# Window attention and a PReLU feed-forward on one Trainium2 core: the mask of four pairs as an identity product in PSUM, and another order of tile 0's products on TensorE

## The chip, the core and the metric

The kernel runs on one core of a Trainium2 chip. Its engines have queues of their own and run each in program order: TensorE (PE, with the weight loads listed as PEld), VectorE (DVE), ScalarE (ACT), GpSimd (POOL), and SyncE (SP), which here only issues DMAs. [...] The metric is the device time of one execution in microseconds (us); a median of several runs is given. The profile is of one execution.

## What is computed

First attention with a window, for 8 batches, 8 heads, 576 positions and 64 channels a head. The first four heads see the last 32 positions, the other four every fourth of the last 128:

```python
mask_plain = (rel >= 0) & (rel < window)
mask_dil = (rel >= 0) & (rel < window * dilation) & (rel % dilation == 0)
scores = np.where(masks[None, :, :, :], scale * (q @ k.T), -1000000000.0)
attn = softmax(scores)
x = attn @ v            # reshaped to 4608 tokens x 512
```

Then a feed-forward layer on all 4608 tokens, in float32:

```python
h = x @ w_in                                             # 512 -> 2048
g = np.maximum(h, 0.0) + alpha * np.minimum(h, 0.0)
out = g @ w_out                                          # 2048 -> 512
```

## The kernel before

**Attention** is done in 32 *pairs* (a batch and two heads; class `Pair`), four pairs to a batch. Positions are laid out so that both kinds of window become blocks of 32 queries by 64 keys, and a pair is nine such blocks on 128 partitions, 576 columns in all. `scores` makes them on PE into two PSUM banks (five blocks and four). `maxima` (DVE) scales them and adds the mask (L194, out to `pr`), and takes the negative maximum of each row (L197), once for each bank. `exponentials` (ACT, L204) makes nine exponentials with their row sums. `divisions` and `turns` (DVE, L211 to L219) divide and transpose in blocks. `values` (PE, L232) multiplies by the values into two banks. `highs` (ACT, L268) and `lows` (DVE, L273) write the result as a rounded part and the remainder, since every float32 product of the feed-forward is made as three products of such parts.

**The feed-forward** goes through the tokens in tiles of 512 and the 2048 channels in 16 slices of 128. For a slice: `ffn_h` (PE, L341, 12 products) into one bank; `ffn_relu` (ACT, L349 and L350); `ffn_sum` (DVE, L355), which is the last reader of the h bank; `ffn_high` (ACT, L368) and `ffn_low` (DVE, L373) make the two parts of g; `ffn_y` (PE, L388, 12 products) adds into four banks that stay for the tile.

**Weights** come as float64 and are converted: a DMA (L288 or L290), a magnitude on ACT (L308), four word operations on DVE (L314 to L320), then `high` on ACT (L326) and `low` on DVE (L329). There are 32 of them, and the list `wq` gives their order; `taken` says how many conversions are begun at the end of each step. A conversion begun in one step has its words made in the next and its low part in the one after.

**PSUM** has eight banks, under two names: y0 to y3 and a0 to a3. `bank(side, ...)` hands them out in turn, and a new tile in a bank waits for the last reader of the old one. Scores of pairs 0 to 4 (`p <= NC`, with `NC` 4) take y banks, and those of later pairs, all values and all h take a banks.

**The order of the work** is written out by hand, for each engine the order of the calls in the program. At the start, loads of the first pairs, masks and weights are issued. A loop over s = 0 to 3 (the first four pairs) makes maxima and exponentials of pair s, one weight conversion beside them, divisions and transposition, scores of pair s+2 and values of pair s. Then come pair 4's maxima and exponentials and the first two slices' h. A loop over n = 0 to 5 then does slice n of tile 0 (`CUT` 6 slices) beside the scores of pair 5+n and the values of pair 4+n. In a step n of that loop before the change, PE gets: scores of pair 5+n, values of pair 4+n, h of slice n+1, and at the end y of slice n-1. DVE gets: the sum of slice n, maxima of pair 5+n, the low part of slice n, conversion words, lows of pair 4+n, low parts of weights, divisions and transposition of pair 5+n. ACT gets: the cast of slice n, five exponentials of pair 5+n, highs of pair 4+n, the other four exponentials, the relu of slice n+1, casts and magnitudes of weights. After this loop, from n = 6, a loop goes on with tile 1's slices, h of slice n+1 and y of slice n-1 in each step, with no pairs until n = 20. At n = 6 the first six slices' sums are copied out (L398 and L400) through DRAM, and slice 6 starts new ones.

Of the kernel before, what the change touches and what calls it, by code (L numbers as in the profile page):

```python
# [7 lines left out]

F32 = mybir.dt.float32
F32R = mybir.dt.float32r  # L10
U32 = mybir.dt.uint32
AF = mybir.ActivationFunctionType
ALU = mybir.AluOpType

P = 128
# [6 lines left out]
BK = 2 * BQ  # L22
HB = 9
HQ = HB * BQ
CUT0 = 5
# [3 lines left out]
NC = DM // P  # L29
NF = DFF // P  # L30
# [8 lines left out]
CUT = 6  # L39


NMASK = 18
PLAIN, DILATED = 0, 9
NEG = -1.0e30
SCALE = 1.0 / D ** 0.5
# [6 lines left out]
def tile_window_attention_prelu_ffn(  # L52
# [11 lines left out]
    nc = tc.nc  # L64
    PS = bass.MemoryType.PSUM

    const = ctx.enter_context(tc.tile_pool(name="const", bufs=1))
# [9 lines left out]
    mask_sb = const.tile([P, NMASK, BK], F32, name="mask_sb")  # L77
# [11 lines left out]
    def bank(side, shape, name):  # L89
        n = turn[side]  # L90
        turn[side] = n + 1
        return psp.tile(shape, F32, tag=f"{side}{n % 4}", name=name)
# [12 lines left out]
    def place(i, k, dtype=F32R):  # L105
        return const.tile([P, SPANS[k][1] - SPANS[k][0], DM], dtype, tag=f"w{i}_{k}", name=f"w{i}_{k}_{dtype}")

    def weight(which, a, f):
        k = next(k for k in range(3) if f < SPANS[k][1])
        i = 2 * which + a  # L110
        if (i, k) not in places:
            places[i, k] = place(i, k)
        return places[i, k][:, f - SPANS[k][0], :]
# [3 lines left out]
    rooms = [place(i, 2, F32).rearrange("p f n -> p (f n)") for i in range(4)]  # L117
    spare_st = [place(i, 1, U32).rearrange("p f (n w) -> p (f n) w", w=2) for i in range(4)]
    vsize = (HB + 1) * D
    taken = 2 * S + vsize  # L120
    spare_pr = [rooms[i][:, taken:taken + HB * BK].rearrange("p (r k) -> p r k", r=HB) for i in range(2)]
    spare_a = [rooms[i][:, taken:taken + DM].bitcast(U32) for i in (2, 3)]


    cells = {}
# [21 lines left out]
    class Pair:  # L147
        def __init__(self, b, c):
            self.b, self.c = b, c
            p = b * NC + c  # L150
            self.banks = "y" if p <= NC else "a"
            self.plain = 2 * c < HP
            self.mask = PLAIN if self.plain else DILATED
            self.id = f"{b}_{c}"
            self.pr = spare_pr[p % 2] if b < 2 else pr0
            self.room = rooms[c] if b < 2 else None
            self.sm = sums[p % 2]

        def load_qk(self):
# [16 lines left out]
        def scores(self):  # L176


            self.ps = [bank(self.banks, [P, n, BK], f"s_{self.id}_{i}") for i, n in enumerate((CUT0, HB - CUT0))]
            for j in range(HB):  # L180
                for u in range(2):
                    for e in range(2):
                        rows, m, n = slice(e * D, (e + 1) * D), 2 * e + u, u * HB + j
                        keys = self.k[rows, (n - 1) * BQ:(n + 1) * BQ] if n else (
                            self.k[rows, None, :BQ].broadcast_to([D, 2, BQ]))
                        nc.tensor.matmul(  # L186
                            self.ps[j // CUT0][m * BQ:(m + 1) * BQ, j % CUT0, :], lhsT=self.q[rows, n * BQ:(n + 1) * BQ],
                            rhs=keys, start=True, stop=True)

        def maxima(self, between=()):  # L190
            between = list(between)
            self.nm = sml.tile([P, HB], F32, tag="nm", name=f"nm_{self.id}")
            for i, (a, z) in enumerate(((0, CUT0), (CUT0, HB))):
                nc.vector.scalar_tensor_tensor(  # L194
                    out=self.pr[:, a:z], in0=self.ps[i], scalar=SCALE, in1=mask_sb[:, self.mask + a:self.mask + z],
                    op0=ALU.mult, op1=ALU.add)
                nc.vector.tensor_reduce(  # L197
                    out=self.nm[:, a:z], in_=self.pr[:, a:z], axis=mybir.AxisListType.X, op=ALU.max, negate=True)
            for op in between:
                op()  # L200

        def exponentials(self, a=0, z=HB):
            for r in range(a, z):
                nc.scalar.activation(  # L204
                    out=self.pr[:, r, :], in_=self.pr[:, r, :], func=AF.Exp,
                    bias=self.nm[:, r:r + 1], scale=1.0, accum_out=self.sm[:, r:r + 1],
                )

        def divisions(self):
# [126 lines left out]
    def ffn_h(t, f, first=0, end=NC):  # L336
        if first == 0:
            ms[t, f] = bank("a", [P, TT], f"h_{t}_{f}")
        for c in range(first, end):
            for n, (a, e) in enumerate(PASSES):  # L340
                nc.tensor.matmul(  # L341
                    ms[t, f], lhsT=weight(0, a, f)[:, c * P:(c + 1) * P], rhs=half(t, c)[:, e, :],
                    start=(c == 0 and n == 0), stop=(c == NC - 1 and n == 2))

    def ffn_relu(t, f):

        ps = ms[t, f]
        m = ffp.tile([P, TT], F32, tag="m", name=f"m_{t}_{f}", bufs=5)
        nc.scalar.activation(out=m, in_=ps, func=AF.Relu, scale=-1.0)  # L349
        nc.scalar.activation(out=ps, in_=ps, func=AF.Relu)  # L350
        ms[t, f] = ps, m

    def ffn_sum(t, f):
        ps, m = ms[t, f]
        nc.vector.scalar_tensor_tensor(  # L355
            out=m, in0=m, scalar=nal[:, f:f + 1], in1=ps, op0=ALU.mult, op1=ALU.add)
        ms[t, f] = m
# [406 lines left out]
    slices = [(0, f) for f in range(CUT)] + [(1, f) for f in range(NF)] + [(0, f) for f in range(CUT, NF)]  # L764
# [5 lines left out]


    wq = [(0, 0), (0, 1), (1, 0)]
    for f in range(1, NF):
        wq += [(0, f + 1), (1, f)] if f + 1 < NF else [(1, f)]
    order.update({w: i for i, w in enumerate(wq)})
    loads, convs = list(wq), list(wq)

    def load():
        if loads:
            load_weight(*loads.pop(0))  # L780

    def conversion():

        w = Conversion(*convs.pop(0))
        w.magnitude()
        return w
# [17 lines left out]
    pairs[2].load_v()  # L804
    pairs[3].load_v()
    pairs[0].scores()
    pairs[1].scores()
    before = conversion()
    for op in before.words():
        op()  # L810
    before.high()
    for s in range(NC):
        u = pairs[s]
        pairs[s + NC].load_qk()
        load()
        if s == 0:
            u.maxima()
            u.exponentials(0, 3)
            w = conversion()
            u.exponentials(3)  # L820
            nc.vector.tensor_scalar_mul(nal, al, -1.0)
            nc.vector.tensor_scalar(out=bal, in0=al, scalar1=-1.0, scalar2=1.0, op0=ALU.mult, op1=ALU.add)
            for op in w.words():
                op()
            before.low()
        else:
            u.maxima(w.words())
            u.exponentials()
            pairs[s - 1].highs()
        w.high()  # L830
        u.divisions()
        if s + 1 == NC:
            ffn_h(0, 0, 0, 2)
        u.turns()
        later = conversion()
        if s + 2 <= NC:
            pairs[s + 2].scores()
        if s:
            pairs[s - 1].lows()
        w.low()  # L840
        w = later
        u.values()
        pairs[s + NC].load_v()
# [15 lines left out]
    load()  # L859
    late, now = [w], [conversion()]  # L860

    taken = [1, 2, 1, 1, 1, 2] + [1, 1, 2, 1, 1, 1, 2, 1, 1, 2, 1, 2, 1]

    def ahead():
        while taken and len(convs) - taken[0] < len(loads):
# [2 lines left out]
    for n in range(CUT):  # L868
        scored = pairs[NC + 1 + n] if n + 1 < NC else None
        valued = pairs[NC + n] if n < NC else None  # L870
        if n == 0:
            for f in range(2):
                ffn_sum(*slices[f])
            valued.divisions()
            valued.turns()
        elif n > 1:
            ffn_sum(*slices[n])
        if scored:
            scored.scores()
        if valued:  # L880
            valued.values()
        if n:
            ffn_h(*slices[n + 1])
        ffn_high(*slices[n])
        if scored:
            scored.maxima()
            scored.exponentials(0, 5)
        ffn_low(*slices[n])
        if valued:
            valued.highs()  # L890
        if scored:
            scored.exponentials(5)
        if n:
            ffn_relu(*slices[n + 1])
        for w in now:
            for op in w.words():
                op()
        if valued:
            valued.lows()
        for w in late:  # L900
            w.low()
        if scored:
            scored.divisions()
            scored.turns()
        for w in now:
            w.high()
        late, now = now, [conversion() for _ in range(taken.pop(0))]
        ahead()
        if n:
            ffn_y(*slices[n - 1])  # L910

    score_at, value_at = {}, {}
    for p in range(2 * NC, AHEAD):
        n = EARLY + 2 * (p - 2 * NC)
# [5 lines left out]
    for k in range(NFP):  # L920
        n = SCRATCH + 1 + 2 * k + (2 if k > 1 else 0)
# [143 lines left out]
```

## Time and profile before

| | |
|---|---|
| median of 3 runs | 895.48 us (895.02 to 897.18) |
| the profiled execution | 895.02 us, span 892.9 us |
| mean granted TensorE clock | 0.98 |
| busy: PE, PEld | 853.4 us (96% of the span), 706.5 us (79%) |
| busy: DVE, ACT, POOL | 561.3 us (63%), 394.3 us (44%), 46.9 us (5%) |
| DMA, mean over the span | 170 GB/s |

Busy shares are means over stages that differ. The page also cuts the span into 40 slices of 22.3 us each, and there PE is busy for 4, 6, 6 and 8 tenths in the first four, and for nine or more in nearly all others. A row of the timeline gives start, length, engine, line, operation, what is written and read, and in brackets the idle time of the engine before it and what ended it. "Issue" there is a wait for which the profile shows no releaser.

### The profile page before, as it was taken

The numbers are of one execution on the slowest core, as the hardware profiler recorded it, in microseconds if no ns is written. First come the engines' busy times: TensorE is split into PE (matmuls) and PEld (weight loads), VectorE is DVE, ScalarE is ACT, GpSimd is POOL, SyncE is SP. The second block draws the span as 40 slices with busy tenths as digits, with TensorE's granted clock in tenths as the row PEclk, the third lists the DMA queues.
The fourth block names the chain that finished last, engine by engine and source line by source line (L and its number), as shares of the span: only waits on it lengthen the run. The fifth ranks groups of instructions, "written<-read, shape, count | busy, mean of one in ns | idle before, by whom it ended". The sixth has DMA issues, their size and how long they took to land.

```text
span 892.9 us, 19710 instructions
## 1 busy us (share of the span) xinstructions
PE 853.4 (96%) x8048; PEld 706.5 (79%) x8048; DVE 561.3 (63%) x964; ACT 394.3 (44%) x1118; POOL 46.9 (5%) x52
## 2 busy tenths in 40 slices
PE   4668999999999999999999999999999999999998
PEld 4556888888888788888888878888788888888886
DVE  6988799976767677675437655764366537304721
ACT  5566466542533444464336442653255226204600
POOL 0000000020223350000000000000000000000000
PEclk9669999999999999999999999999999999999999
DMA  9612245216889965565556555655365466436631
GB/s 344 219 59 94 86 151 174 80 47 193 253 273 334 301 201 175 188 190 162 156 166 193 173 178 174 195 162 162 96 192 158 148 179 194 124 98 172 180 128 47
DMA packets 101448, 151.81 MB, mean 170 GB/s; under 512 B 8432, under 2 KB 47344, under 8 KB 101360
## 3 DMA queue, kind: packets, MB, share of 16 engines
q1 hardware_dynamic: 101360, 150.58, 54.9%
q8 instruction: 63, 1.03, 0.5%
q14 instruction: 25, 0.20, 0.1%
HBM read 116.99 MB, written 33.55 MB: 169 GB/s over the span
## 4 chain that ended last, share of the span: by engine, by line
PE 94%; DVE 2%; issue 2%; ACT 1%; DMA 0%; SPq 0%; DVEq 0%; ACTq 0%
PE y L676 30%; PE h L341 15%; PE pA L538 15%; PE y L388 15%; PE pC L538 7%; PE o L232 5%; PE pB L538 4%; PE s L186 3%; ACT w_dt.float L204 1%; DMA ws<-w_in 0%; DVE pt L219 0%; DVE w_dt.float L213 0%; DVE w_dt.float32r L329 0%; DVE nm L197 0%; DVE wa L318 0%
## 5 line engine op out<-in xcount | busy, mean ns | idle before, releaser
L341 PE MATMUL h<-x,w_dt.float32r 128*128 128x512 f32 x576 | 144.4, 400 | 1.6 <-issue 1.6
L388 PE MATMUL y<-g,w_dt.float32r 128*128 128x512 f32 x576 | 138.4, 389 | 0.0
L341 PEld LDWEIGHTS h<-x,w_dt.float32r 128*128 128x128 f32 x576 | 109.6, 193 | 25.2 <-issue 1.8
L388 PEld LDWEIGHTS y<-g,w_dt.float32r 128*128 128x128 f32 x576 | 108.0, 188 | 22.5
L676 PE MATMUL y<-gp,ring_w 128*128 128x512 f32 x480 | 112.3, 390 | 0.0
L676 PEld LDWEIGHTS y<-gp,ring_w 128*128 128x128 f32 x480 | 89.7, 188 | 18.9
L676 PE MATMUL y<-gp,ring_xA 128*128 128x512 f32 x444 | 103.8, 390 | 0.0
L676 PEld LDWEIGHTS y<-gp,ring_xA 128*128 128x128 f32 x444 | 83.0, 188 | 17.5
L204 ACT ACTIVATE pr<-pr,nm 128x64 f32<-128x64 f32 x216 | 72.2, 336 | 47.2 <-DVE nm L197 47.2
L580 ACT COPY stage<-pA 128x512 f32<-128x512 f32 x72 | 42.3, 587 | 105.2 <-PE pA L538 105.2
L606 DVE TENSOR_TENSOR gp<-n,gp 128x512 fp32r<-128x512 f32 x96 | 63.1, 683 | 0.0
L368 ACT CAST g<-m 128x512 fp32r<-128x512 f32 x48 | 29.7, 619 | 75.4 <-DVE m L363 69.2
L598 DVE SCALAR_TENSOR_TENSOR n<-n,bal,stage 128x512 f32<-128x512 f32 x72 | 53.9, 748 | 13.6 <-ACT n L594 12.8
L538 PE MATMUL pA<-parts_w,ring_w 128*128 128x512 f32 x234 | 57.7, 390 | 0.7 <-ACT raw_xA L268 0.7
L602 ACT CAST gp<-n 128x512 fp32r<-128x512 f32 x96 | 56.6, 615 | 1.8 <-DVE n L598 1.8
L538 PE MATMUL pA<-parts_w,ring_xA 128*128 128x512 f32 x228 | 56.2, 390 | 0.5 <-ACT raw_xB L268 0.5
L676 PE MATMUL y<-gp,ring_g 128*128 128x512 f32 x228 | 54.5, 391 | 0.0
L699 DVE TENSOR_TENSOR ob<-y,py 128x512 f32<-128x512 f32 x24 | 16.4, 690 | 57.8 <-PE y L676 57.8
L538 PEld LDWEIGHTS pA<-parts_w,ring_w 128*128 128x128 f32 x234 | 43.9, 188 | 9.9 <-ACT raw_xA L268 0.8
L594 ACT ACTIVATE n<-stage 128x512 f32<-128x512 f32 x72 | 45.6, 633 | 12.5 <-DVE stage L587 11.9
L538 PEld LDWEIGHTS pA<-parts_w,ring_xA 128*128 128x128 f32 x228 | 42.7, 188 | 9.5 <-ACT raw_xB L268 0.6
L676 PEld LDWEIGHTS y<-gp,ring_g 128*128 128x128 f32 x228 | 42.5, 188 | 9.1
(97 smaller groups left out, 1147.3 us busy)
## 6 DMA issues: line engine op xcount, KB each, us to landing
ring_w<-wS SPq DMA_DIRECT2D x68, 256.0 KB, 2.9
ring_xA<-wS SPq DMA_DIRECT2D x67, 256.0 KB, 2.9
ring_w<-wO SPq DMA_DIRECT2D x40, 256.0 KB, 2.7
ring_xA<-wO SPq DMA_DIRECT2D x37, 256.0 KB, 2.7
out<-ob SPq DMA_DIRECT2D x36, 256.0 KB, 2.9
ring_g<-wS SPq DMA_DIRECT2D x33, 256.0 KB, 2.9
wO<-w_dt.float32r SPq DMA_DIRECT2D x32, 256.0 KB, 5.0
wS<-wc SPq DMA_DIRECT2D x16, 512.0 KB, 3.7
```

The source lines that it names most:

```text
L204: nc.scalar.activation(out=self.pr[:, r, :], in_=self.pr[:, r, :], func=AF.Exp, bias=self.nm[:, r:r + 1], scale=1.0, accum_out=self.sm[:, ...
L232: nc.tensor.matmul(self.po[u][e * D:(e + 1) * D, a:z, :], lhsT=self.v[rows, i, :], rhs=self.pt[rows, a * BK + (BQ if i else 0):z * BK - (B ...
L341: nc.tensor.matmul(ms[t, f], lhsT=weight(0, a, f)[:, c * P:(c + 1) * P], rhs=half(t, c)[:, e, :], start=(c == 0 and n == 0), stop=(c == NC ...
L368: nc.scalar.copy(out=g[:, 0, :], in_=ms[t, f])
L388: nc.tensor.matmul(ys[t][c], lhsT=weight(1, a, f)[:, c * P:(c + 1) * P], rhs=g[:, e, :], start=(first and n == 0), stop=(last and n == 2),)
L538: nc.tensor.matmul(to, lhsT=w[:, (2 * a + c) * P:(2 * a + c + 1) * P], rhs=part_of(name, e)[:, c * TT:(c + 1) * TT], start=start and c == ...
L580: nc.scalar.copy(out=self.s(n), in_=self.A)
L594: nc.scalar.activation(out=self.m[n], in_=self.at(n), func=AF.Relu, scale=-1.0)
L598: nc.vector.scalar_tensor_tensor(out=self.m[n], in0=self.m[n], scalar=bal[:, f:f + 1], in1=self.at(n), op0=ALU.mult, op1=ALU.add)
L602: nc.scalar.copy(out=self.g(n)[:, 0], in_=self.m[n])
L606: nc.vector.tensor_tensor(out=g[:, 1], in0=self.m.pop(n), in1=g[:, 0].bitcast(F32), op=ALU.subtract)
L676: nc.tensor.matmul(ys2[tt], lhsT=w[:, k * P:(k + 1) * P], rhs=g[:, e], start=j == 0 and n == 0, stop=j == GF - 1 and n == 2)
```

## The change

It has two parts.

*The mask.* For pairs 1 to 4 (`self.onto`) the mask isn't added on DVE. It is written once as rounded float32 (`added`, two copies on ACT), an identity matrix is made on POOL and copied on ACT (`unit_r`), and a product of the two opens each score bank; the score products then add to it. The maxima are taken from PSUM and multiplied by the scale afterwards (two small operations more), and the exponentials read PSUM and write `pr`. So the y banks of these pairs are held until their exponentials have been read.

*The order.* In step n of the loop over tile 0's slices, PE now gets scores of pair 5+n, y of slice n-1, h of slice n+2, and then the values of pair 4+n. The sum on DVE and the relu on ACT are issued for slices n+1 and n+2. The order of the weights and the number of conversions begun in the first steps follow.

```diff
+    added_all = const.tile([P, NMASK + 2, BK], F32R, tag="xC0", name="added")
+    added = {kind: added_all[:, kind:kind + HB] for kind in (PLAIN, DILATED)}
+    unit_r = added_all[:, NMASK:].rearrange("p j k -> p (j k)")
+    unit = rooms[0][:, taken + HB * BK:taken + HB * BK + P]
+    make_identity(nc, unit)
...
+            self.onto = 1 <= p <= NC
...
+            if self.onto:
+                for i, (a, z) in enumerate(((0, CUT0), (CUT0, HB))):
+                    nc.tensor.matmul(
+                        self.ps[i], lhsT=unit_r, rhs=added[self.mask][:, a:z],
+                        start=True, stop=False, skip_group_check=True)
...
-                            rhs=keys, start=True, stop=True)
+                            rhs=keys, start=not self.onto, stop=True, skip_group_check=self.onto)
...
-                nc.vector.scalar_tensor_tensor(
-                    out=self.pr[:, a:z], in0=self.ps[i], scalar=SCALE, in1=mask_sb[:, self.mask + a:self.mask + z],
-                    op0=ALU.mult, op1=ALU.add)
+                if not self.onto:
+                    nc.vector.scalar_tensor_tensor(
+                        out=self.pr[:, a:z], in0=self.ps[i], scalar=SCALE, in1=mask_sb[:, self.mask + a:self.mask + z],
+                        op0=ALU.mult, op1=ALU.add)
                 nc.vector.tensor_reduce(
-                    out=self.nm[:, a:z], in_=self.pr[:, a:z], axis=mybir.AxisListType.X, op=ALU.max, negate=True)
+                    out=self.nm[:, a:z], in_=self.ps[i] if self.onto else self.pr[:, a:z],
+                    axis=mybir.AxisListType.X, op=ALU.max, negate=True)
+                if self.onto:
+                    nc.vector.tensor_scalar_mul(self.nm[:, a:z], self.nm[:, a:z], SCALE)
...
-                    out=self.pr[:, r, :], in_=self.pr[:, r, :], func=AF.Exp,
-                    bias=self.nm[:, r:r + 1], scale=1.0, accum_out=self.sm[:, r:r + 1],
+                    out=self.pr[:, r, :], in_=self.ps[r // CUT0][:, r % CUT0, :] if self.onto else self.pr[:, r, :],
+                    func=AF.Exp, bias=self.nm[:, r:r + 1], scale=SCALE if self.onto else 1.0,
+                    accum_out=self.sm[:, r:r + 1],
...
-    for f in range(1, NF):
-        wq += [(0, f + 1), (1, f)] if f + 1 < NF else [(1, f)]
+    wq += [(0, 2), (0, 3), (1, 1), (0, 4), (1, 2), (0, 5), (1, 3), (1, 4), (1, 5)]
+    for f in range(CUT, NF):
+        wq += [(0, f), (1, f)]
...
     pairs[0].scores()
+    before = conversion()
+    nc.scalar.copy(out=unit_r, in_=unit)
+    nc.scalar.copy(out=added[PLAIN], in_=mask_sb[:, PLAIN:PLAIN + HB])
     pairs[1].scores()
-    before = conversion()
...
         later = conversion()
+        if s == 0:
+            nc.scalar.copy(out=added[DILATED], in_=mask_sb[:, DILATED:DILATED + HB])
...
-    taken = [1, 2, 1, 1, 1, 2] + [1, 1, 2, 1, 1, 1, 2, 1, 1, 2, 1, 2, 1]
+    taken = [2, 1, 1, 1, 1, 2] + [1, 1, 2, 1, 1, 1, 2, 1, 1, 2, 1, 2, 1]
...
         if n == 0:
-            for f in range(2):
-                ffn_sum(*slices[f])
+            ffn_sum(*slices[0])
+            ffn_sum(*slices[1])
             valued.divisions()
             valued.turns()
-        elif n > 1:
-            ffn_sum(*slices[n])
+        elif n + 1 < CUT:
+            ffn_sum(*slices[n + 1])
         if scored:
             scored.scores()
+        if n:
+            ffn_y(*slices[n - 1])
+        if n + 2 <= CUT:
+            ffn_h(*slices[n + 2])
         if valued:
             valued.values()
-        if n:
-            ffn_h(*slices[n + 1])
         ffn_high(*slices[n])
...
-        if n:
-            ffn_relu(*slices[n + 1])
+        if n + 2 <= CUT:
+            ffn_relu(*slices[n + 2])
...
         ahead()
-        if n:
-            ffn_y(*slices[n - 1])
```

`make_identity` is a helper: a memset and an `affine_select` on POOL.

More of the change, by code (lines that the diff above doesn't have):

```diff
@@ L7 @@
 from concourse._compat import with_exitstack
+from concourse.masks import make_identity
 F32 = mybir.dt.float32
```

## The prediction

> **What bounds the kernel now.** I read the header of the page first, then a table of the windows at the start, then the chain of waits over the first 150 us.
>
> ```profile
> span 892.9 us, 19710 instructions
> ```
>
> The profiled execution took 895.02 us, 2.1 us more than its span; the median of the three runs is 895.48 us. My sum is a shift of the profiled execution, and what lies around the span stays as it is.
>
> ```profile
> 50.00:80.00 30.00, 21.29 (x420) 18.10 (x420) 27.38 (x61) 21.11 (x82) 0.00 (x0) 0.77 0.21 63
> 88.00:106.00 18.00, 18.00 (x82) 14.89 (x81) 14.86 (x27) 10.33 (x21) 0.00 (x0) 1.00 0.19 68
> ```
>
> The columns are stretch, length, then busy time of PE, PEld, DVE, ACT and POOL, granted clock, DMA. In the first stretch of 30 us PE is busy for 21.3 us, at a mean clock of 0.77, and DVE for 27.4: DVE sets the pace, and PE has gaps. In the second PE is busy throughout, at full clock. So whatever the change does is decided before that, in the stage where four first-stage pairs and tile 0's six slices are done. The question is when PE's unbroken run begins, and whether DVE and ACT can then feed it.
>
> **The mask in PSUM.** The chain of waits shows one whole round, pair 1's (start, length, what):
>
> ```profile
> 17.23 0.41 DVE w_dt.float L194
> 17.67 0.50 DVE nm L197
> 18.19 3.10 ACT w_dt.float L204 x18
> 21.32 0.18 DVE rs L211
> 21.52 0.23 DVE rs L212
> 21.77 0.77 DVE w_dt.float L213
> 22.64 0.78 DVE pt L219
> 23.42 0.77 DVE x L273 x3
> 24.19 0.59 DVE w_dt.float32r L329
> ```
>
> Each of pairs 1 to 4 loses the two mask additions on DVE and gains two small multiplications of the maxima.
>
> ```profile
> L194 DVE SCALAR_TENSOR_TENSOR w_dt.float<-s,mask_sb x16: 412/434/490, 9.1 to 71.6; 128x320 f32<-128x320 f32 x8, 128x256 f32<-128x256 f32 x8
> ```
>
> Removed: 2 x 0.43 = 0.87 us. Added: two operations spaced like the small dependent ones at L211 and L212, 21.52 - 21.32 = 0.20 each, so 0.4. DVE gains about 0.45 us a pair, and the first exponential starts some 0.25 earlier. The exponentials now read PSUM in place of SBUF. No row shows that for L204; the nearest are two operations of one size, from PSUM (L349) and from SBUF (L308), mean ns last:
>
> ```profile
> L349 ACT ACTIVATE m<-h 128x512 f32<-128x512 f32 x8 | 4.7, 593 | 14.8 <-PE h L341 14.8
> ...
> L308 ACT ACTIVATE wa<-w_dt.uint 128x512 f32<-128x512 f32 x6 | 4.0, 664 | 0.0
> ```
>
> That is 0.07 us less; the bounds are 0 and 0.07, I take 0.04, and nine make 0.36. The conversion that DVE does beside the exponentials shortens too, so a round becomes about 0.55 us shorter. Three rounds (pairs 1 to 3) give 1.65, pair 4's later exponentials and the gaps between them 0.35: **2.0 us earlier** at the end of this part. Its bounds: 3.0 (0.25 + 9 x 0.07 for each of three rounds, and pair 4) and -0.5, if the maxima become dearer from PSUM and the score products are late.
>
> [...]
>
> What covers the rest: the identity is two POOL operations in the first microseconds, when POOL has nothing else; two copies on ACT stand behind the first magnitude. A third, of the dilated mask, waits for its transfer.
>
> ```profile
> L789 SPq DMA_DIRECT2D mask_sb<-masks x2: 430/468/505, 2.1 to 7.8; - x2
> ...
> DMA to landing us min/median/max: 4.9/6.6/8.3
> ```
>
> The second mask is issued at 7.8 and lands 8.3 later, at 16.1 (the first can't take 8.3, it is used at 9.1). So pair 2's scores come at about 17 and not at 12.4, and pair 0's values behind them on PE some 3 us later. Those values are next needed when pair 1's exponentials are done (18.19 + 3.10 = 21.3), so this costs nothing up to about 1 us. Pairs 3 and 4 need a bank that is now held until the exponentials have read it; their scores fall in the 2 us of division and transposition that DVE needs anyway. Eight identity products run where PE waits.
>
> **The new order on TensorE.** PSUM banks a0 to a3 are handed out in turn, and PE waits for a bank's last reader. Two rows show it (the last bracket is the wait):
>
> ```profile
> 38.55 1.31 DVE L273 TENSOR_TENSOR x<-o,x 128x256 fp32r<-128x256 f32 x4
> 39.31 2.24 PEld L232 LDWEIGHTS o<-pt,w_dt.float 32*64 32x64 f32 x76 [4.28 <-issue]
> 39.34 2.35 PE L232 MATMUL o<-pt,w_dt.float 32*64 32x32 f32 x76 [3.88 <-issue]
> ...
> 48.64 1.21 PE L186 MATMUL s<-w_dt.float 64*32 64x64 f32 x72 [1.28 <-DVE m L355]
> ```
>
> Pair 3's values began when the first half of L273, the reader of their bank, was done; pair 5's scores began after slice 0's L355. Count the turns after the change: pair 5's scores a2 and a3, h of slice 2 a0, pair 4's values a1 and a2, **pair 6's scores a3 and a0**, h of slice 3 a1, pair 5's values a2 and a3, **pair 7's scores a0 and a1**. So the second half of pair 6's scores waits until slice 2's sum (L355) has read a0. That sum stands on DVE behind pair 5's whole round, and behind the waiting product on PE stand y 0, h 3 and pair 5's values. The same comes again with pair 7 and slice 3. Before, a pair's scores took banks that were long free. DVE in turn waits for the values (subtractions L273, then division, transposition, next sum): each engine waits for the other.
>
> ```profile
> 53.08 0.45 DVE L194 SCALAR_TENSOR_TENSOR w_dt.float<-s,mask_sb 128x320 f32<-128x320 f32 x1
> ...
> 60.95 0.45 DVE L194 SCALAR_TENSOR_TENSOR w_dt.float<-s,mask_sb 128x320 f32<-128x320 f32 x1
> ```
>
> A round of DVE is 7.87 us. It begins 2.0 earlier, at 51.1, and slice 2's sum ends at 51.1 + 7.9 + 0.7 = 59.7. From there PE does half the scores, y, h and values:
>
> ```profile
> 69.83 1.21 PE L186 MATMUL s<-w_dt.float 64*32 64x64 f32 x72
> 70.97 1.35 PE L232 MATMUL o<-pt,w_dt.float 32*64 32x32 f32 x76
> 72.26 3.02 PE L341 MATMUL h<-x,w_dt.float32r 128*128 128x512 f32 x12
> 75.12 2.88 PE L388 MATMUL y<-g,w_dt.float32r 128*128 128x512 f32 x12
> ```
>
> By starts, 0.6 + 2.8 + 2.7 + 1.3 = 7.4 us at full clock. But PE has idled since values 4, which end at about 54 (51.1 + 0.5 for the L194 that reads their bank + 2.35 at most), and this is what an idle stretch does (the columns as above):
>
> ```profile
> 78.00:82.00 4.00, 0.53 (x35) 0.56 (x38) 3.89 (x10) 0.79 (x2) 0.00 (x0) 1.00 0.46 133
> 82.00:86.00 4.00, 4.00 (x62) 3.37 (x55) 3.22 (x6) 1.85 (x5) 0.00 (x0) 0.57 0.02 4
> ```
>
> After 3.5 us without work the clock was 0.57 for 4 us, which loses about 1.7. I take 2.3 lost after the first, longer gap (bounds 0 and 3.4), and 1.7 after the second. So values 5 end at 59.7 + 7.4 + 2.3 = 69.4. Then 0.75 for the casts, 4 x 0.34 for exponentials queued behind them on ACT, 2.0 for division and transposition, 0.7 for slice 3's sum: 74.2. Second time: 74.2 + 7.4 + 1.7 = 83.3, the end of values 6.
>
> [...]
>
> **From there to the steady run.** Pair 6's casts and subtractions end 1.7 later; y 2 needs a weight whose low part DVE makes behind them, at 2.4. Then 2.3 for the rest of y, 2.7 for h 5, 1.3 for values 7: 8.7. Subtractions and another low part: 11.0, which y 3 waits for; with 2.3 and 2.7, h 6 ends at 16.1. The relu is now issued two slices ahead, and in ACT's queue slice 5's cast (L368) stands behind h 6's relu: about 0.55 each for the relu's two operations and 0.6 for two conversions and the cast (as at L349 and L308), 19.0. DVE waits for that cast; low part, four conversion words (2.3) and a low part: slice 6's sum starts at 22.5, so at 83.3 + 22.5 = 105.8.
>
> ```profile
> 99.42 0.75 DVE L355 SCALAR_TENSOR_TENSOR m<-m,nal,h 128x512 f32<-128x512 f32 x1 [0.36 <-ACT h L350]
> ...
> 105.79 0.68 DVE L398 COPY ob<-y 128x512 f32<-128x512 f32 x1
> ...
> 113.14 0.68 DVE L373 TENSOR_TENSOR g<-m,g 128x512 fp32r<-128x512 f32 x1
> ...
> 114.36 2.88 PE L388 MATMUL y<-g,w_dt.float32r 128*128 128x512 f32 x12
> ```
>
> Before, that sum was at 99.42, the sums' copy 6.4 later, slice 7's low part done at 113.82, and its y on PE at 114.36, with 0.5 to spare. PE was the later one. Now DVE is: the sum is 6.4 us later, less those 0.5 and 0.2 of rounding, so y of slice 7 is about 5.7 later, and PE runs without a gap from there on. The extra conversion moved from n=2 to n=1 changes no total; the new load order moves the same transfers, each still loaded a step ahead.
>
> **Sum:** 895.02 + 5.7 = **900.7 us**, of which -2.0 is in it from the mask. For the forecast alone 898.3 to 903.
>
> **Rivals.**
> *Clock stays up* (chance 0.22): the gaps fall so that no cold time follows, which takes 2.3 + 1.7 = 4.0 off: 896.7. For it: 54 to 60 is the only gap far above 3.5 us. Against it: the row at 82.
> *No held bank, not slower* (0.14): if the second half of pair 6's and pair 7's scores is not held, values 5 come with the end of pair 5's round at 59.0 (51.1 + 7.9), DVE runs on, and the same working puts slice 6's sum at about 97.3, 2.1 early: 893.0; if slice 5's cast isn't late either, 890. It decides once PE reaches values 5 before DVE has finished the next words, about 66. Against it stand the rows at 39.34 and 48.64; for it, DVE's 27.4 busy of 30, which leaves little to lose.
> *The mask gains nothing* (0.14): the longer held banks put pair 3's and 4's scores in the way of the values, 0.6 to 1 us a round, and the 2.0 is given back; or one more gap of 2 us lets the clock fall (1.7). 902.7 to 904.4.
>
> **Chances.** Forecast 0.50. About 0.3% (2.7 us) is what a measurement of this kernel can tell from no change. Faster by more: most of the no-hold case and a little of the clock case, 0.13. Within: the rest of these, 0.27. Slower: forecast and the last rival, less the forecast's edge, 0.60. The range, 892.5 to 904.5, leaves out half of the no-hold case and the upper end of the last.
>
> **What would show it.** Right: pair 5's first L194 near 51 and not 53.1; a PE gap of some 4 us inside pair 6's scores and one inside pair 7's, ended by L355; eight L194 fewer; DVE waiting on L268 before pair 5's and 6's L273; slice 6's sum later than 99.4. Wrong: values 5 before 62, no wait inside the scores, or PE unbroken from 60 on.

## The result, and the profile after

The changed kernel took **903.08 us** (median of four runs, 901.72 to 904.97) against 895.29 of the kernel before beside it: a ratio of 1.0084, 95% interval 1.0061 to 1.0107. It is slower by 7.8 us; the forecast was 900.7, 5.4 above that median, with a range of 892.5 to 904.5. Its profiled execution took 903.32 us, 8.3 more than that of before. The header of its page:

```profile
span 901.5 us, 19731 instructions
```

Where the time went shows in one row each of the table of windows, for the stretch from 50 to 118 us, in which tile 0's slices are done (columns as in the prediction). Before:

```profile
50.00:118.00 68.00, 57.82 (x645) 48.51 (x646) 57.88 (x115) 40.49 (x120) 0.00 (x0) 0.87 0.26 86
```

After:

```profile
50.00:118.00 68.00, 50.29 (x610) 39.14 (x609) 50.05 (x101) 34.59 (x109) 0.00 (x0) 0.91 0.19 63
```

PE is busy for 7.5 us less of the 68, DVE for 7.8 less and ACT for 5.9 less, at a granted clock that is on average no lower (0.91 for 0.87). No engine has more to do (over the whole span PE is busy for 853.9 us and was for 853.4, DVE for 559.5 and 561.3, ACT for 394.3 in both): all three wait for one another. The end of the disturbance is slice 7's y on PE, which stood at 114.36 and now begins at 122.55, 8.2 later; the spans differ by 8.6. So nearly all of the loss is made before this point.

The waits themselves, from the timeline of PE after the change (L198 are scores, L405 y, L358 h, L249 values; the last bracket is the wait before the row and what ended it):

```profile
54.37 0.76 PE L198 MATMUL s<-w_dt.float 64*32 64x64 f32 x40
61.21 1.08 PE L198 MATMUL s<-w_dt.float 64*32 64x64 f32 x32 [6.08 <-DVE m L372]
62.22 4.01 PE L405 MATMUL y<-g,w_dt.float32r 128*128 128x512 f32 x12
66.07 2.89 PE L358 MATMUL h<-x,w_dt.float32r 128*128 128x512 f32 x12
68.89 1.35 PE L249 MATMUL o<-pt,w_dt.float 32*64 32x32 f32 x76
...
75.06 1.08 PE L198 MATMUL s<-w_dt.float 64*32 64x64 f32 x32 [4.12 <-DVE m L372]
...
86.68 2.56 PE L405 MATMUL y<-g,w_dt.float32r 128*128 128x512 f32 x10 [2.02 <-DVE w_dt.float32r L346]
...
95.94 2.58 PE L405 MATMUL y<-g,w_dt.float32r 128*128 128x512 f32 x10 [2.03 <-DVE w_dt.float32r L346]
```

Pair 6's scores are split: 40 products at 54.37, the other 32 after a wait of 6.08 us for L372, which is the sum on DVE (L355 before). The same comes again in pair 7's scores, 4.12 us. These are the two held banks. Later y 2 and y 3 each wait 2.0 us for a weight's low part (L346). The other side of each wait is in DVE's timeline:

```profile
60.45 0.71 DVE L372 SCALAR_TENSOR_TENSOR m<-m,nal,h 128x512 f32<-128x512 f32 x1
...
70.66 0.89 DVE L290 TENSOR_TENSOR x<-o,x 128x288 fp32r<-128x288 f32 x3 [2.33 <-ACT x L285]
...
74.30 0.70 DVE L372 SCALAR_TENSOR_TENSOR m<-m,nal,h 128x512 f32<-128x512 f32 x1
...
84.68 1.35 DVE L290 TENSOR_TENSOR x<-o,x 128x224 fp32r<-128x224 f32 x4 [4.75 <-ACT x L285]
...
104.05 0.69 DVE L390 TENSOR_TENSOR g<-m,g 128x512 fp32r<-128x512 f32 x1 [3.54 <-ACT g L385]
...
107.51 0.74 DVE L372 SCALAR_TENSOR_TENSOR m<-m,nal,h 128x512 f32<-128x512 f32 x1
```

DVE does slice 2's sum at 60.45, at the end of its round; 0.05 us after its end at 61.16 PE goes on. Then DVE waits for ACT's casts of the values (L285). PE could make these values only after that sum, and slice 3's sum comes behind them on DVE. Slice 6's sum is at 107.51 (99.42 before). Before, its longest wait between 51 and 100 us was this one, of 1.15 us:

```profile
70.67 0.49 DVE L194 SCALAR_TENSOR_TENSOR w_dt.float<-s,mask_sb 128x320 f32<-128x320 f32 x1 [1.15 <-PE s L186]
```

### The profile page after: what moved, and what is told of

It is laid out like the page before. It is cut to its first block, busy times and chain, and to the rows that moved or that the text cites. A ratio compares the mean times of both kernels' runs of the same rounds, so it can differ in the third digit from the quotient of the medians.

```text
span 901.5 us, 19731 instructions
## 1 busy us (share of the span) xinstructions
PE 853.9 (95%) x8056; PEld 702.9 (78%) x8056; DVE 559.5 (62%) x964; ACT 394.3 (44%) x1121; POOL 47.4 (5%) x54
## 3 DMA queue, kind: packets, MB, share of 16 engines
q8 instruction: 64, 1.05, 0.5%
## 4 chain that ended last, share of the span: by engine, by line
PE 91%; DVE 4%; ACT 3%; issue 1%; DMA 1%; SPq 0%; ACTq 0%; DVEq 0%
PE y L693 29%; PE pA L555 15%; PE y L405 14%; PE h L358 14%; PE pC L555 7%; PE o L249 4%; PE pB L555 4%; PE s L198 4%; ACT w_dt.float L220 1%; DMA ws<-w_in 1%; DVE w_dt.float32r L346 1%; DVE pt L236 0%; DVE w_dt.float L230 0%; DVE x L290 0%; DVE m L372 0%
## 5 line engine op out<-in xcount | busy, mean ns | idle before, releaser
L405 PE MATMUL y<-g,w_dt.float32r 128*128 128x512 f32 x576 | 143.4, 398 | 6.9 <-DVE w_dt.float32r L346 4.6
L358 PE MATMUL h<-x,w_dt.float32r 128*128 128x512 f32 x576 | 141.8, 395 | 2.1 <-issue 1.7
L405 PEld LDWEIGHTS y<-g,w_dt.float32r 128*128 128x128 f32 x576 | 109.5, 192 | 32.4 <-DVE w_dt.float32r L346 5.9
L358 PEld LDWEIGHTS h<-x,w_dt.float32r 128*128 128x128 f32 x576 | 107.7, 189 | 25.6 <-issue 2.7
```

Source lines behind the costliest of these rows:

```text
L358: nc.tensor.matmul(ms[t, f], lhsT=weight(0, a, f)[:, c * P:(c + 1) * P], rhs=half(t, c)[:, e, :], start=(c == 0 and n == 0), stop=(c == NC ...
L405: nc.tensor.matmul(ys[t][c], lhsT=weight(1, a, f)[:, c * P:(c + 1) * P], rhs=g[:, e, :], start=(first and n == 0), stop=(last and n == 2),)
```

## The experiments

Theory: the two held banks make the loss; the mask in PSUM saves about 2 us by itself. Rivals: the mask part costs time and the order is harmless; the loss is the cold clock after the waits (granted 0.50 from 58 to 62 us and 0.71 from 62 to 66 in the changed kernel); or it is the order on PE (y and h ahead of the values) whatever the banks. Each ratio is against the kernel before in the same set of runs.

| kernel | median us | ratio, 95% interval |
|---|---|---|
| mask_only | 892.86 | 0.9970 (0.9952 to 0.9987) |
| order_only | 904.08 | 1.0099 (1.0067 to 1.0130) |
| banks | 894.78 | 1.0001 (0.9984 to 1.0017) |
| early_sum | 897.59 | 1.0029 (1.0009 to 1.0050) |
| after_again | 902.50 | 1.0066 (1.0049 to 1.0084) |
| banks_cast | 895.47 | 0.9996 (0.9980 to 1.0011) |
| values_first | 893.41 | 0.9962 (0.9947 to 0.9977) |
| h_in_gap | 890.13 | 0.9923 (0.9904 to 0.9941) |
| after_warm | 904.63 | 1.0101 (1.0076 to 1.0127) |
| hgap_warm_a | 893.04 | 0.9975 (0.9957 to 0.9993) |
| hgap_warm_b | 888.84 | 0.9928 (0.9902 to 0.9955) |
| h_in_gap_again | 889.60 | 0.9930 (0.9904 to 0.9956) |

The kernel before stood at 895.1 in the first four, 896.6 in the next four and 895.0 in the last four.

### The two halves apart

**mask_only** keeps the mask in PSUM and takes the order, the weights' order and the conversions of before:

```diff
-        if n:
-            ffn_y(*slices[n - 1])
-        if n + 2 <= CUT:
-            ffn_h(*slices[n + 2])
         if valued:
             valued.values()
+        if n:
+            ffn_h(*slices[n + 1])
...
+        if n:
+            ffn_y(*slices[n - 1])
...
```

> The changed kernel with the order of before on TensorE, the old weight order and the old conversion counts; only the mask by an identity product stays. If the mask is worth what the three rounds in the trace of after show (6.97 us each against 7.6), it comes to 893.0 us, 2.3 below before, give or take 1. If the first weight's landing, 6.7 us in the trace of after against 4.4, belongs to the mask part, it comes to 895 and the landing is late again. If the mask gives nothing, 895.3.

**order_only** keeps the new order and adds the mask on DVE, as before:

```diff
-            self.onto = 1 <= p <= NC
+            self.onto = False
...
```

> The changed kernel with the mask added on DVE as before; only the new order, weight order and conversion counts stay. By the theory of the held banks it carries the whole loss and lacks the mask's gain: 905.5 us, 10 above before (904 to 907), with two waits of 4 to 6 us inside the scores of pairs 6 and 7, ended by the slice's sum. If part of the loss in after comes from the mask (banks held for the exponentials), it is below after's 903.

Measured: 2.2 us less for the mask alone, 9.0 more for the order alone; together 6.8, where both at once gave 7.8 and, in a second set, 5.9. So the two add up within the scatter, and the rival that the mask part costs time is out: in mask_only's trace, too, slice 7's y begins 1.6 us earlier than before (112.75 for 114.36). The same wait stands in the order's own timeline of PE:

```profile
62.93 1.08 PE L193 MATMUL s<-w_dt.float 64*32 64x64 f32 x32 [6.07 <-DVE m L367]
```

What the mask saves shows in the timeline of ACT, in the first exponentials of pairs 1 and 2. Before:

```profile
18.19 0.35 ACT L204 ACTIVATE w_dt.float<-w_dt.float,nm 128x64 f32<-128x64 f32 x1 [2.85 <-DVE nm L197]
...
18.54 0.33 ACT L204 ACTIVATE w_dt.float<-w_dt.float,nm 128x64 f32<-128x64 f32 x1
...
18.87 0.33 ACT L204 ACTIVATE w_dt.float<-w_dt.float,nm 128x64 f32<-128x64 f32 x1
...
25.80 0.35 ACT L204 ACTIVATE w_dt.float<-w_dt.float,nm 128x64 f32<-128x64 f32 x1 [2.81 <-DVE nm L197]
```

After:

```profile
20.24 0.31 ACT L220 ACTIVATE w_dt.float<-s,nm 128x64 f32<-128x64 f32 x1 [2.05 <-DVE nm L214]
...
20.55 0.30 ACT L220 ACTIVATE w_dt.float<-s,nm 128x64 f32<-128x64 f32 x1
...
20.84 0.31 ACT L220 ACTIVATE w_dt.float<-s,nm 128x64 f32<-128x64 f32 x1
...
27.21 0.31 ACT L220 ACTIVATE w_dt.float<-s,nm 128x64 f32<-128x64 f32 x1 [2.01 <-DVE nm L214]
```

A round was 25.80 - 18.19 = 7.61 us and is 6.97: 0.64 less, where 0.55 was forecast. One exponential follows the next after 0.29 us in place of 0.33. The maxima, by groups of line and shape after the change (columns as on the page, mean ns second to last):

```profile
L210 DVE TENSOR_REDUCE nm<-w_dt.float 128x5 f32<-128x320 f32 x4 | 2.0, 488 | 0.1
L210 DVE TENSOR_REDUCE nm<-s 128x5 f32<-128x320 f32 x4 | 1.9, 486 | 0.0
```

A maximum from PSUM (`s`) took 486 ns, one from SBUF 488. So the 0.04 us that the forecast took off for an exponential from PSUM is what the rows of ACT show, 0.33 less 0.29; a dearer maximum, which it had as a bound, they don't show.

### The held banks alone

**banks** is the changed kernel with other numbers for eight of the tiles in the a banks (of the ten in the list, 23 and 27 keep theirs), so that no half of a pair's scores follows an h whose sum is still to come. No instruction is added, taken away or moved:

```diff
+    SWAPS = {16: 1, 17: 0, 20: 1, 21: 2, 22: 0, 23: 3, 24: 1, 25: 2, 26: 0, 27: 3}
...
-        return psp.tile(shape, F32, tag=f"{side}{n % 4}", name=name)
+        k = SWAPS.get(n, n % 4) if side == "a" else n % 4
+        return psp.tile(shape, F32, tag=f"{side}{k}", name=name)
```

> The changed kernel with every engine's order kept; only the numbers of the a banks from pair 6's second score bank to pair 7's values are dealt out otherwise, so that no scores land on the bank of an h whose sum is still to come. Held-bank theory: the second half of pair 6's scores waits for pair 4's subtractions only (about 3.7 us sooner), pair 7's for pair 5's (about 3 sooner), DVE's waits before L290 shrink, and the time is 896 us (894.5 to 898). Rival, that y and h ahead of the values on TensorE are the cause by themselves: it stays at 902 to 904.

```profile
54.60 0.65 PE L200 MATMUL s<-w_dt.float 64*32 64x64 f32 x32 [2.48 <-DVE x L292]
...
65.37 0.65 PE L200 MATMUL s<-w_dt.float 64*32 64x64 f32 x32 [2.17 <-DVE x L292]
...
77.25 4.08 PE L407 MATMUL y<-g,w_dt.float32r 128*128 128x512 f32 x10 [2.02 <-DVE w_dt.float32r L348]
...
88.02 2.58 PE L407 MATMUL y<-g,w_dt.float32r 128*128 128x512 f32 x10 [2.02 <-DVE w_dt.float32r L348]
```

In its timeline of PE the waits inside the scores are 2.48 and 2.17 us, and end with a subtraction of the values (L292), which DVE does in the middle of its round, and no longer with the sum at the round's end. That takes the whole loss back: -0.3 us against before, where the changed kernel had +7.8 and +5.9. So the two held banks cost 6 to 8 us. The rival that the order as such makes the loss keeps the rest: banks is 1.9 above mask_only (their intervals just meet), and the two waits of 2.02 for a weight's low part are unchanged. Nor does the clock make the difference: in banks, too, y 1 behind the wait of 2.17 us took 4.61 us (granted clock 0.61 from 66 to 70 us), and y 2 4.08 for ten products (0.68 from 78 to 82).

**early_sum** frees the bank in another way: the relu of slice n+2 goes ahead of pair 5+n's exponentials on ACT, and its sum behind the maxima on DVE.

```diff
-        elif n + 1 < CUT:
-            ffn_sum(*slices[n + 1])
...
             scored.maxima()
+            ffn_relu(*slices[n + 2])
+            ffn_sum(*slices[n + 2])
             scored.exponentials(0, 5)
...
```

> The changed kernel with the relu of slice n+2 ahead of pair 5+n's exponentials on ACT and its sum right behind that pair's maxima on DVE, so that the h bank is read before the pair's division. Held-bank theory: no wait inside the scores, values of pair 5 by 63 us, time 893.5 us (891 to 896). Rival, that the order on TensorE is the cause by itself: 901 or more.

This missed: 897.59 for 893.5, between the two cases of the expectation. Its timeline of PE has no wait inside the scores, and values 5 begin at 59.22, as expected. But further on:

```profile
78.55 4.63 PE L405 MATMUL y<-g,w_dt.float32r 128*128 128x512 f32 x10 [3.61 <-DVE w_dt.float32r L346]
...
86.66 1.35 PE L249 MATMUL o<-pt,w_dt.float 32*64 32x32 f32 x76
```

y 2 waits 3.61 us for a low part, values 7 stand behind it and h 5 until 86.66, and ACT waits 9.48 us for them. ACT also waits 3.94 us for slice 4's h with the exponentials behind it. So the early sum takes away the wait that it was meant for, and others take its place; that they make up the 2.5 us above the kernel before is read from this trace and not tested.

**values_first** leaves the banks' turns and puts the values ahead of y and h:

```diff
+        if valued:
+            valued.values()
         if n:
             ffn_y(*slices[n - 1])
         if n + 2 <= CUT:
             ffn_h(*slices[n + 2])
-        if valued:
-            valued.values()
```

> The changed kernel with the values put back ahead of y and h on TensorE; h stays two slices ahead, and the banks are dealt out in turn again, which now gives the scores banks that are free. Held-bank theory, and the theory that values must not stand behind y: no waits inside the scores, DVE nearly without gaps from pair 5 on, 889 us (887.5 to 891.5). If being two slices ahead costs something by itself (the relu on ACT ahead of the cast), 892 to 895.

```profile
59.82 1.35 PE L249 MATMUL o<-pt,w_dt.float 32*64 32x32 f32 x76 [0.92 <-DVE m L372]
...
70.59 1.35 PE L249 MATMUL o<-pt,w_dt.float 32*64 32x32 f32 x76 [2.63 <-DVE m L372]
```

Values 5 begin at 59.82 in place of 68.89, values 6 at 70.59 in place of 82.64. They still wait for a sum, but 0.92 and 2.63 us, with nothing ahead of them. The time was 893.41, not the 889 of the better case: 0.9962 against 0.9970 for mask_only. So with the values first, h two slices ahead does no harm and brings nothing that can be measured; with h and y ahead of the values, and the banks in turn, the order cost 9 us.

**after_again** is the changed kernel unaltered, to see how much of the 7.8 is chance.

> The changed kernel once more, unaltered, for the scatter of its start. If the late landing of the first weight (6.7 us in the trace of after, 4.4 in that of before) is chance, this profile has another landing, about 5 to 6, and the median is 901 to 902.5; the second slice-7 y comes as much earlier as the landing. If it belongs to the change, it is again 6.7 or more, and the median 903.

It gave 902.50, 5.9 above the kernel before. Its timeline of PE:

```profile
59.16 1.08 PE L198 MATMUL s<-w_dt.float 64*32 64x64 f32 x32 [6.08 <-DVE m L372]
60.16 4.90 PE L405 MATMUL y<-g,w_dt.float32r 128*128 128x512 f32 x12
...
74.49 4.58 PE L405 MATMUL y<-g,w_dt.float32r 128*128 128x512 f32 x12
...
95.00 4.12 PE L405 MATMUL y<-g,w_dt.float32r 128*128 128x512 f32 x10 [2.02 <-DVE w_dt.float32r L346]
```

It stood 2.05 us earlier at the first held bank (59.16 for 61.21), with a wait of the same 6.08. By slice 7's y the lead was gone (122.72 for 122.55): the three y after waits took 0.89, 0.66 and 1.54 us longer. Equal waits had unequal aftermaths, and that the two executions stood 0.17 us apart in the end is chance. The expectation that the lead would last to slice 7's y was wrong.

**banks_cast** is banks with slice 5's cast (`ffn_high`) issued ahead of slice 6's relu, since DVE waits 3.54 us for that cast.

```diff
-        ffn_high(*slices[n])
+        if n < CUT - 1:
+            ffn_high(*slices[n])
...
+        if n + 2 == CUT:
+            ffn_high(*slices[n + 1])
```

> As banks, and in step 4 the cast of slice 5 stands ahead of the relu of slice 6 on ACT. If that place in ACT's queue costs what the trace of banks shows (DVE waits 3.5 us for the cast at L392), slice 6's sum and the copies of the sums come about 3 us sooner and the time is 892.3 us (891 to 893.5). If DVE's wait only moves to another place, it stays at 894 to 895.

It gave 895.47, 0.9996 against 1.0001: nothing that can be told from none. DVE's wait for the cast is gone, and the next row waits for a magnitude that stands behind the same relu:

```profile
94.57 0.68 DVE L392 TENSOR_TENSOR g<-m,g 128x512 fp32r<-128x512 f32 x1
...
97.67 0.43 DVE L333 TENSOR_SCALAR w_dt.float<-w_dt.float 128x512 f32<-128x512 f32 x1 [2.42 <-ACT w_dt.float L327]
```

### The clock alone

**after_warm** fills the two waits inside the scores: the first half of pair 6's scores is written eight times, that of pair 7 six times, so that PE doesn't idle.

```diff
+            for _ in range({'1_2': 7, '1_3': 5}.get(self.id, 0)):
+                self.products(0, CUT0)
+            self.products(0, HB)
```

> The changed kernel, but the first half of pair 6's scores is written eight times in place of once and that of pair 7 six times (the same products into the same bank, 0.72 us each, so 5.0 and 3.6 us of the waits of 6.1 and 4.1 us inside these scores are filled). Nothing else moves. It takes the cold clock after the two waits away and leaves the waits. Theory (part of the loss is the clock): y of slices 0 and 1 take 2.9 to 3.0 us in place of 4.0 to 4.9 and 3.9 to 4.6, the rest of the scores 0.65 in place of 1.08, and since VectorE then waits for the values this is passed on: 3 to 4 us less, 898.5 to 899.5 against the 902.5 to 903.1 of the changed kernel. Rival (VectorE is the bound there and the clock costs nothing): 902 to 903. If the repeated products hold back the maxima of the pair, it would be above 903.

```profile
53.51 1.98 PE L203 MATMUL s<-w_dt.float 64*32 64x64 f32 x126
56.79 1.99 PE L203 MATMUL s<-w_dt.float 64*32 64x64 f32 x128 [1.30 <-issue]
61.62 1.64 PE L203 MATMUL s<-w_dt.float 64*32 64x64 f32 x98 [2.83 <-issue]
63.18 3.06 PE L410 MATMUL y<-g,w_dt.float32r 128*128 128x512 f32 x12
```

The clock did stay up: it was 1.00 from 58 to 66 us, and y 0 took 3.06 us in place of 4.01 and 4.90. (This trace is of the fastest of its runs, 901.91 us.) But the repeated products came with two pauses of 1.30 and 2.83 us for which the trace names no releaser. They ended late, and DVE waited 2.55 us for pair 6's scores. y 0 so began at 63.18, and h 3 at 66.08, where it had begun at 66.07. The time, 904.63, is that of the third case in the expectation, and the test doesn't price the clock. What the cold clock costs is read from the rows alone: from the second part of pair 6's scores to h 3 the changed kernel took 66.07 - 61.21 = 4.86 us and 5.75 in the second execution, against 3.59 in banks (58.19 - 54.60), where the granted clock was 1.00 from 54 to 62 us and y 0 took 3.02: 1.3 to 2.2 us.

### A version that is faster than both

**h_in_gap** is mask_only, with the next slice's h (one ahead, as before) ahead of the values in two of the six steps:

```diff
+        if n in (1, 3):
+            ffn_h(*slices[n + 1])
         if valued:
             valued.values()
-        if n:
+        if n and n not in (1, 3):
             ffn_h(*slices[n + 1])
```

> mask_only, with h of the next slice ahead of the values in steps 1 and 3 alone, where its trace shows TensorE idle for 3.5 us before the values. If these gaps are what holds the time, the two gaps are filled and the half clock after the second goes: 889.5 us (888 to 891.5). If DVE is the bound anyway, 892 to 893.

> h_in_gap unaltered, beside the two kernels that are built from it: 890.1, within 1, and about 0.992 of the kernel before.

890.13 and 889.60: 0.7 to 0.8% below the kernel before, and with intervals below that of mask_only in the first set, and meeting its edge in the second. The row of windows that stands above for before and after:

```profile
50.00:118.00 68.00, 61.10 (x661) 49.79 (x662) 60.82 (x121) 43.12 (x123) 0.00 (x0) 0.92 0.27 90
```

PE is busy for 61.1 of the 68 us and DVE for 60.8: both more than in either kernel. Yet this kernel has a held bank, too. In the second set's trace the second half of pair 7's scores waits 3.09 us for slice 2's sum, longer than the scores in banks waited (2.48 and 2.17):

```profile
66.91 0.65 PE L198 MATMUL s<-w_dt.float 64*32 64x64 f32 x32 [3.09 <-DVE m L372]
```

Here the values come right behind, at 67.49, with no y and h between. In the first set's trace that wait is 1.83 us, and DVE's longest wait from 55 to 95 us is 0.69 us. So a wait of this kind need not cost anything; it matters what stands behind it.

**hgap_warm_a** and **hgap_warm_b** add repeated scores to it in a gap of PE, ahead of pair 3's and of pair 4's values:

```diff
         w = later
+        if s + 1 == NC:
+            pairs[NC].products(0, HB)
         u.values()
```

> As h_in_gap (890.13), but pair 4's scores are written twice, the second time just ahead of pair 3's values, where TensorE waited 2.7 us. If the cold clock after that wait matters, the first two slices' h (18 products, 5.75 us there and 4.4 in other executions) take 4.4, VectorE's waits for them (1.9 and 1.7 us) are shorter together by about 1.3, and the time is 888.5 to 889. If the time after this point is set elsewhere, as the wait for slice 6's sum suggests: 890, within 0.5.

```diff
             scored.scores()
+        if n == 0:
+            scored.products(0, HB)
+            scored.products(0, HB)
```

> As h_in_gap (890.13), but pair 5's scores are written three times, which fills 2.4 of the 3.2 us that TensorE waits ahead of pair 4's values. These values, pair 6's scores and slice 2's h then run at full clock (1.35, 1.21 and 2.9 us in place of 2.35, 2.15 and 4.71). Theory (VectorE, busy 3.83 to 3.90 of every 4 us from 50 to 74, is the bound there): no gain, 890, within 0.7. Rival (TensorE's clock is the bound there): about 3 us less, 887.

The second gave 888.84, no different from h_in_gap, as it would be if DVE sets the pace there. It is a weak test: slice 2's h took 3.03 us in its trace in place of 4.71 in h_in_gap's, but 3.03 in h_in_gap_again's too, without any repeats; and the trace is of its slowest run, 893.59 us. The first gave 893.04, 3.4 above h_in_gap beside it. Its trace does not carry a loss in this part: slice 7's y begins at 108.40, and at 108.51 in h_in_gap_again, and the spans of 890.9 and 888.5 part only afterwards, at waits of PE that stand at other places of the two programs. In hgap_warm_a:

```profile
261.45 3.02 PE L361 MATMUL h<-x,w_dt.float32r 128*128 128x512 f32 x12 [2.12 <-DVE ob L416]
...
522.26 0.21 PE L201 MATMUL s<-k,q 64*32 64x64 f32 x1 [1.68 <-issue]
```

In h_in_gap_again:

```profile
275.64 3.59 PE L358 MATMUL h<-x,w_dt.float32r 128*128 128x512 f32 x8 [1.73 <-issue]
```

Why they stand there isn't shown. So a difference of 2 to 3 us between these kernels need not come from the place where they were changed.

## Why the prediction held

**"The mask in PSUM ... 2.0 us earlier": right.** Alone it is worth 2.2 us (interval of the ratio 0.9952 to 0.9987). The round is 0.64 shorter for 0.55. The bound of -0.5, maxima dearer from PSUM, is excluded by 486 against 488 ns. L207 (L194 before) has eight instructions fewer.

**"Pair 6's scores a3 and a0 ... waits until slice 2's sum": right, and nearly the whole loss.** Both pairs' scores wait on L372 in their middle; the sum forecast to end at 59.7 and the next at 74.2 ended at 61.16 and 75.00, and the first one at 59.10 in the second execution. Pair 5's first addition, forecast at 51.1, was at 52.58, and at 50.53 in the second execution. Against the kernel before, the first weight landed 2.3 us later. ACT's first magnitude, before:

```profile
6.10 0.67 ACT L308 ACTIVATE wa<-ws 128x512 f32<-128x512 f32 x1 [4.09 <-DMA ws<-w_in]
```

After:

```profile
8.40 0.66 ACT L325 ACTIVATE wa<-ws 128x512 f32<-128x512 f32 x1 [6.39 <-DMA ws<-w_in]
```

In the second execution ACT could start at 7.86, only 0.54 earlier than at 8.40. The rest of its lead of 2.05 us is in two rows of PE: pair 3's values and the first two slices' h took 1.35 and 4.40 us in place of 1.83 and 5.47, where the first execution had a granted clock of 0.68 (39.79 to 41.60) and 0.79 (41.55 to 47.00). The forecast had put neither in, and the second is chance, since the two executions are of one program.

The gap in PE, "some 4 us", was 6.1 and 4.1. Freeing the banks and nothing else took 6 to 8 us back.

**The clock terms, 2.3 and 1.7.** The 1.7 was taken from the row at 82; the 2.3 was the author's estimate between bounds of 0 and 3.4, and no run shows it. Measured by the rows: 1.3 to 2.2 after the first wait, and 75.06 to 79.82 for h 4 after the second, 4.76, 1.2 above the 3.59 of banks; 4.99 in the second execution, 1.4 above. Both a little smaller than put. The granted clock of the changed kernel was 0.68 from 61.20 to 66.10 us and 0.69 from 75.06 to 79.80. The rival "clock stays up" came in neither execution: y 0 took 4.01 and 4.90 us, y 1 3.92 and 4.58. After waits of 2.02 and 2.03 us ten products of y took 4.12 us in the second execution and 2.58 in the first (granted clock 1.00 from 95.90 to 98.50); what decides between the two isn't shown.

**From values 6 to slice 6's sum: the step that was too small.** It was put at 22.5 us; from the end of values 6 at 83.99 to 107.51 it was 23.5 us, and in the second execution, with these 4.12 us for y 3, 25.1. The waits for the two low parts, put at 2.4 and 2.3 behind the values, came out at 2.7 (83.99 to 86.68, 93.24 to 95.94). From that sum to slice 7's y the forecast was 14.3 (the 14.9 of before less 0.5 and 0.2); it was 15.0, since slice 6's y waited on PE for the copies of the sums, 2.08 and 0.23 us, which the sum had left out. The forecast had DVE as the later of the two at slice 7's y; the low part of slice 7 was done on DVE at 121.76, and PE came to its y at 122.55, so PE was the later one again, as before the change. So 1.0 and 0.8 us here, and 0.7 by which values 6 already ended later than the forecast's 83.3 (the later start, less what the clock cost less): that is the 2.5 between the 8.2 at slice 7's y and the forecast's 5.7.

**The rivals.** "No held bank" was priced at 893.0, or 890 with the cast in time; the experiment that makes it so gave 894.78, and 895.47 with the cast ahead: the price of the bank was right to 2 us, and the cast was worth nothing, because the magnitude behind it is late as well. "The mask gains nothing", 902.7 to 904.4, holds the measured time, but its mechanism is excluded by mask_only: the time came there because the order cost 9.0 and not 7.7.

## What to carry to other kernels

Where buffers are handed out in turn, moving a product ahead moves the turn of every buffer behind it: write down, for each new tile, who reads the old one last and where that reader stands in its own queue. A wait placed inside a queue holds up what stands behind it; here, at waits of 6.08 and 4.12 us, the values behind a product that nobody needed yet fed the engine whose work the wait was for. Before an order is given up, try other buffers for the same order, which moves no instruction and tells the two causes apart.

## What was not expected of the hardware

- In after_warm the long runs of small products had pauses in them. Pair 6's scores came as 126, 128 and 98 products (each with a weight load) with 1.30 and 2.83 us between them and no releaser in the trace. The trace counts 67 packets and 1.10 MB on the queue "instruction" in place of 64 and 1.05 MB; the repeats are 480 products, with their loads 960 instructions more than in the changed kernel. What the pauses come from isn't shown.
- The first weight's transfer let ACT start at 6.10 us in the one trace of the kernel before, and at 6.71 to 8.40 in those of the others; whether the change moves it isn't shown. It doesn't settle where tile 0's slices begin: h_in_gap had 6.95 and then 7.76, but pair 4's values at 52.52 and then 50.55. What differed was PE's time for pair 3's values and the first two h, 2.34 and 5.75 us, and then 1.35 and 4.40. Nor does a lead of 2 us there settle the end: the spans of these two are 888.7 and 888.5. 1.5 us of it went at about 276 us, where the same pause of 1.73 us was followed by eight products of h in 2.11 us and in 3.59.
- In the changed kernel an exponential of 64 columns that read PSUM followed the last after 0.29 us, one that read SBUF after 0.33, while a maximum of 320 columns took 486 and 488 ns.
